# Two third sums on VectorE, one instruction each in place of three, and a new written order of the jobs

## The chip, the core and the metric

The kernel runs on one core of a Trainium2 chip. The metric is the device time of one execution in microseconds, the median of several runs. TensorE (PE in the profile) multiplies matrices, VectorE (DVE) and ScalarE (ACT) work on elements, GpSimd (POOL) and SyncE (SP) mostly issue DMAs here.

## The reference

Two independent parts are written side by side into one output of 2048 rows and 2 x 576 columns.

```
q, k, v = split(x @ wqkv)                       # 32 heads of 18 columns
logits[s, w] = q[s] . k[s - 2w] / sqrt(18)      # w = 0..7, masked where s < 2w
a = softmax_w(logits) ; A = (sum_w a[s, w] v[s - 2w]) @ wo
kv = (k shifted and weighted by 4 taps) * v     # B's own q, k, v
y  = irfft(rfft(pad(kv)) * rfft(pad(ssm_k)))[:2048] + kv * ssm_D
B  = q * y
out = concat(A, B)
```

## The kernel before

Part A is a local dilated attention, part B a long convolution by transforms. The convolution is cut into 4 blocks of 512 rows. Each block of x (the product kv) and each block of the filter is turned into a spectrum by matmuls with tables of sines; the spectra of x lie in the tile `xw`, those of the filter in `Ks`. A spectrum has a real and an imaginary half of 2304 columns. A complex product is made with three real products instead of four, so each spectrum also needs a third half, the sum of its first two. For blocks 0 and 1 VectorE makes this third sum (`third_sum`, L939, instruction at L942); for blocks 2 and 3 DMAs do it (`third`, L632: a copy issued on SP at L634, then an adding DMA on POOL at L626).

All work after a fixed start is cut into some 360 jobs. The string `ORDER` (L20 to L37) names them in the order in which their instructions are issued; each engine then executes its own instructions in that order, and waits where its operands or its targets are not ready. Nothing else sets the order. The jobs of which the prediction speaks:

- `q..`, `k..`, `v..`: projections of x (matmuls L322, L326, L333, L339; ScalarE copies the result from PSUM, L355). `T`: taps of block i on VectorE (L517 to L536). `M`: folding (L545, copy L548). `I`: a table (L397). `x i g h`: a unit of the spectrum of x (four matmuls L682, copy L684).
- `Fm`: folds filter block m (matmuls L602, two ScalarE copies L605 into `Ks`, then three adding DMAs on POOL at L607 to L610). `K m c g`: a unit of the filter's spectrum (matmuls L567 and L568, copy L618). `K.1.` reads what the copies L605 wrote, `K.0.` what the adding DMAs left.
- `RG`: ScalarE reorders a block of v's weights, loaded from HBM (L780).
- `L h u c`: VectorE multiplies q by shifted k (L706) into one of three homes (`LHOMES`), and `G h u c` sums over the columns of a head on TensorE (L720). `sm`: softmax.
- `D`: weights spread by DMA; `V n c`: VectorE weighs v (L813) into one of three homes (`VHOMES`), `A n c` adds over w on TensorE (L824, tail L838). `O`: output projection (L888, L880).
- `p j t i`: VectorE multiplies third t of the spectra of x block i and filter block j-i (L950) into one of five homes (`PHOMES`); `z j t i` adds it up on TensorE (L975) and with the last i the result is copied (L988, the very last one by VectorE, L986). `y`: joins two products (L958) for block 3. `i`, `b`, `g`: inverse transform (L1010, L1029), mirrored half (L1059, L1038), multiplication by q (L1075, L1020) and store.
- `ak`, `ax`: the third sums of filter and of x.

PSUM has four slots of two banks. They are handed out in turn (`slots`, L103): a new unit of matmuls takes the slot that was given back first, and must wait until ScalarE has copied what was in it. A home of a product may be written again only when TensorE has read it. A matmul that uses a part of the array (64 rows or columns, 32 columns, a quarter) has another tile shape than a full one; the shape changes often between jobs.

Of the kernel before, what the change touches and what calls it, by code (L numbers as in the profile page):

```python
# [17 lines left out]
PSUM = bass.MemoryType.PSUM  # L18

ORDER = """  # L20
    T0 k03a' T1 S1 k03b I1 k02a k02b Lk2 Lv2 I0 k00a' Lk3 Lv3 M01 X5 k00b q10a Ex q10b Lf3 T2 Lo3 q13a' q13b
    k10a k10b T3 k13a' Lf2 k13b q12a q12b N2 Lo2 k01a M10 k01b Lf1 M00 k11a k11b q11a M11 q11b Lf0 N3 Lw SV L001
    k12a M20 k12b x001 M21 x021 q24a x020 q24b x000 Lo1 k24a Fr Lo0 Z2 N1 RG3 k24b RG2 F3 RG0 F2 L000 K310 G000
    K311 K210 K211 L002 K313 G001 RG4 F1 G002 L003 G003 K302 L004 G004 K301 L010 K212 L011 K303 K213 K203 N0 F0
    L012 K200 K300 G010 L013 K201 K312 K202 RG1 G011 G012 K113 K103 G013 L014 G014 K112 K102 K101 L100 K100 K010
    K111 K110 sm0a K001 K013 sm0b v24a' L101 v24b L102 G100 L103 G101 K012 sm0c sm0d U3 U2 K000 K011 K003 G102
    K002 D0 D1 v11a v11b G103 L104 G104 ak00 M30 v12a' v12b ak02 v01a ak01 L110 G110 M31 L111 G111 v01b v00a'
    L112 G112 L113 Wl v00b G113 x031 U1 L114 G114 V04 v10a' v10b A04 sm1a sm1b v02a v02b v03a' sm1c v03b x201
    V10 V11 sm1d V12 A10 v13a' v13b D2 x330 x310 x301 V13 A11 V20 V21 x200 x331 x230 x010 x221 A20 x321 V22 x210
    x011 V23 D3 V34 ax02 x220 x030 x300 D4 A21 V40 V41 A34 D5 O000' x211 V42 x320 x231 x111 x131 Tx2 A40 V43  # L30
    x120 x101 ax00 x130 ax01 V50 x121 x311 O001 A41 V51 O100' p000 x100 x110 O010 A50 V52 z000 O011' V53 O101
    A51 Tk2 p010 z010 ax10 O020' O021 p020 z020 O110' ak10 i000 p200 i02880 Q0 p100 z100 p101 p110 p111 Q1 z101
    i02881 i001 p121 p120 O111 z110 p201 z111 z120 p210 z121 O120 p211 z200 z210 z211 p212 z212 z201 p202 z202
    Tx3 p220 Tk3 p221 O030' p222 O121 b0288 z220 p301 z221 O031' p302 b00 z222 p303 i200 i100 g0 Q2 p300 y300
    p312 i12880 i201 i101 i12881 z300 z301 z303 p310 p311 y310 O130 b10 b1288 p313 g1 Q3 p322 O131' z310 p320
    z311 p321 z313 i22880 i300 b20 y320 p323 i22881 i301 b2288 g2 z320 z321 z323 b30 i3384L g30 g3384
"""  # L37

LHOMES = (0, 1, 2, 0, 1, 2, 0, 1, 2, 0, 1, 2, 0, 1, 0, 1, 0, 1, 0, 1)
# [6 lines left out]
def view(t, offset, dims):  # L46

    return bass.AP(tensor=t.tensor, offset=t.offset + offset, ap=[list(t.ap[0])] + [list(d) for d in dims])
# [3 lines left out]
def kernel(  # L52
# [42 lines left out]
    HB = 4 * D  # L95
    QTR = 768
# [15 lines left out]
    xw = main.tile([128, 12 * HB], BF16, name="xw")  # L112
# [5 lines left out]
    XG = (9, 0, 3, 6)  # L118
# [49 lines left out]
    Ks = main.tile([128, 12 * HB], BF16, name="Ks")  # L168
# [3 lines left out]
    def k_at(m, part):  # L172
        return 3 * HB * (3 - m) + HB * part
# [87 lines left out]
    for h in range(2):  # L261
        f = fold[:, 64 * h:64 * h + 64]
# [225 lines left out]
    def job(name, fn, *args):  # L488

        assert name not in jobs  # L490
        jobs[name] = partial(fn, *args)
# [444 lines left out]
    todo = [(j, t, i) for j in range(NBL) for t in range(3) for i in range(j + 1)]  # L936
    PRODUCT = (("av", 0), ("v", 6912), ("qk", 9216), ("qk", 9216 + HB), ("Ks", k_at(3, 2)))

    def third_sum(t, at, w):  # L939

        a, b, c = (view(t, at + HB * part, [[1, w]]) for part in range(3))
        tt(c, a, b, ALU.add)  # L942

    def product_home(n):
# [148 lines left out]
    for j in range(NBL):  # L1093
        job(f"Q{j}", load_q, j)
        for c0, n in ((0, HD), (HD, HD)) if j < NBL - 1 else ((0, 2 * TH), (2 * TH, TH)):
            inverse(j, c0, n)
    for t in range(3):
        job(f"ak0{t}", third_sum, Ks, k_at(0, 0) + QTR * t, QTR)
        job(f"ax0{t}", third_sum, xw, HB * XG[0] + QTR * t, QTR)
    job("ak10", third_sum, Ks, k_at(1, 0), HB)  # L1100
    job("ax10", third_sum, xw, HB * XG[1], HB)

    for name in ORDER.split():
        jobs.pop(name.rstrip("'"))(*([True] if name[-1] == "'" else []))
# [31 lines left out]
```

## Time and profile before

| what | value |
|---|---|
| runs shown | 206.28, 206.78, 206.79 us (median 206.78) |
| the profiled execution | 206.3 us, of which the span on the core is 204.6 us |
| granted TensorE clock, mean | 0.994 |
| PE matmuls busy | 196.9 us, 96% of the span, 2074 instructions |
| DVE busy | 192.3 us, 94%, 146 instructions |
| ACT busy | 155.6 us, 76% |
| POOL busy | 60.8 us, 30% |
| DMA | 38.48 MB, mean 188 GB/s |

Times in the views run from the start of the span. A row of the timeline has its start, how long it lasted, engine, line, operation, what is written and read, how many instructions are merged into it, and in brackets the idle time before it with what ended that. An engine's instructions overlap a little at their ends, so what a step costs on a busy engine is read from start to start. Matmuls are pipelined and their ends are modelled, so for PE the starts count too.

### The profile page before, as it was taken

The page shows a single profiled execution, that of the slowest core. Times are in us where ns is not written, and L with a number is a line of the kernel's source. Part 1 is how long each engine was busy: PE and PEld are TensorE (multiplying, and loading weights), DVE is VectorE, ACT ScalarE, POOL GpSimd, SP SyncE. Part 2 cuts the span into 40 slices and gives each one's busy share as a digit, 9 for nine tenths or more (in the row PEclk, how much of TensorE's full clock was granted, in tenths as well). Part 3 has the DMA queues.
Part 4 walks back from the last instruction along what each step waited for, and adds up shares of the span by engine and source line. Part 5 has one row for each costly group of instructions (what it writes and reads, how often), then busy time and mean ns, then how long its engine had stood idle before and what let it go on. Part 6 is the DMA issues. An engine that isn't in the chain of part 4 may idle for free.

```text
span 204.6 us, 5004 instructions
## 1 busy us (share of the span) xinstructions
PE 196.9 (96%) x2074; PEld 109.9 (54%) x2074; DVE 192.3 (94%) x146; ACT 155.6 (76%) x223; POOL 60.8 (30%) x106
## 2 busy tenths in 40 slices
PE   7999999999989999999999999999999999999990
PEld 2543544334455646543245556776666767766660
DVE  7559999999999999999999999999999999899992
ACT  4788995678899999966578678886778767767760
POOL 8989500011348581400380000004090001030300
PEclk9999999999999999999999999999999999999997
DMA  6999899989509869999899990879989303944555
GB/s 197 280 293 306 175 289 373 214 177 281 169 3 146 111 82 185 167 180 222 157 235 216 248 244 34 141 183 334 186 227 233 100 28 122 227 130 145 153 182 150
DMA packets 34916, 38.48 MB, mean 188 GB/s; under 512 B 17523, under 2 KB 28911, under 8 KB 34894
## 3 DMA queue, kind: packets, MB, share of 16 engines
q1 hardware_dynamic: 26668, 24.29, 46.5%
q0 software_dynamic: 5760, 11.36, 29.5%
q10 hardware_dynamic: 2466, 2.51, 3.6%
q8 instruction: 16, 0.26, 0.5%
q14 instruction: 6, 0.05, 0.1%
HBM read 13.11 MB, written 4.72 MB: 87 GB/s over the span
## 4 chain that ended last, share of the span: by engine, by line
PE 88%; DMA 3%; ACT 2%; DVE 2%; issue 1%; SPq 1%; DVEq 0%
PE ps_proj L322 18%; PE ps_fx L682 8%; PE ps_wo L888 8%; PE ps_z L975 8%; PE ps_inv L1010 7%; PE ps_acc L824 7%; PE ps_fk L567 5%; PE ps_log L720 5%; DMA Ks<-in_A_x_dram 3%; PE ps_proj L333 3%; PE ps_proj L326 3%; PE ps_proj L439 3%; PE ps_fk L568 3%; PE ps_fold L545 2%; PE ps_wo L880 1%
## 5 line engine op out<-in xcount | busy, mean ns | idle before, releaser
L322 PE MATMUL ps_proj<-xw 128*128 128x512 bf16 x160 | 38.5, 380 | 0.0
L706 DVE TENSOR_TENSOR av<-qk 128x4096 bf16<-128x4096 bf16 (+1 forms) x16 | 31.7, 2014 | 0.1
L322 PEld LDWEIGHTS <-xw 128*128 128x128 bf16 x160 | 13.9, 98 | 19.4 <-issue 5.7
L988 ACT ACTIVATE av<-ps_z 128x768 bf16<-128x768 f32 x23 | 17.2, 811 | 6.5 <-PE ps_z L975 6.0
L517 DVE TENSOR_TENSOR tB<-kj,skb 128x4608 bf16<-128x4608 bf16 (+1 forms) x8 | 19.3, 2416 | 0.1
L950 DVE TENSOR_TENSOR qk<-xw,Ks 128x2304 bf16<-128x2304 bf16 x14 | 18.9, 1354 | 0.3 <-PE ps_z L975 0.3
L684 ACT ACTIVATE xw<-ps_fx 128x576 bf16<-128x576 f32 x32 | 18.6, 665 | 0.3 <-PE ps_fx L682 0.2
L618 ACT ACTIVATE Ks<-ps_fk 128x576 bf16<-128x576 f32 x32 | 18.6, 699 | 0.2 <-PE ps_fk L568 0.2
L355 ACT ACTIVATE qk<-ps_proj 128x1024 bf16<-128x1024 f32 x14 | 14.3, 1023 | 5.2 <-PE ps_proj L333 2.8
L888 PE MATMUL ps_wo<-qk 128*128 128x288 bf16 x128 | 17.9, 287 | 0.0
L626 POOL DMA_DIRECT2D Ks<-Ks x8 | 10.1, 1426 | 26.0 <-PE ps_back L1059 19.3
L682 PE MATMUL ps_fx<-xw,TB 128*128 128x288 bf16 x128 | 17.7, 287 | 0.0
L567 PE MATMUL ps_fk<-Ks,TB 128*128 128x384 bf16 x62 | 16.5, 327 | 0.1
L824 PE MATMUL ps_acc<-av,ident 64*64 64x512 bf16 x160 | 15.3, 378 | 0.0
L1010 PE MATMUL ps_inv<-av,TI 128*128 128x288 bf16 (+1 forms) x112 | 15.2, 292 | 0.0
L568 PE MATMUL ps_fk<-Ks,TB 128*128 128x192 bf16 x62 | 15.2, 246 | 0.0
L682 PEld LDWEIGHTS <-TB 128*128 128x128 bf16 x128 | 11.9, 98 | 5.9 <-issue 2.7
L888 PEld LDWEIGHTS <-qk 128*128 128x128 bf16 x128 | 11.7, 98 | 5.4 <-issue 2.7
L355 ACT ACTIVATE v<-ps_proj 128x1024 bf16<-128x1024 f32 x9 | 9.3, 1033 | 6.5 <-PE ps_proj L322 4.5
L813 DVE TENSOR_TENSOR av<-Ks,v 128x4096 bf16<-128x4096 bf16 x6 | 13.5, 2286 | 0.0
L827 ACT ACTIVATE qk<-ps_acc 128x1024 bf16<-128x1024 f32 x8 | 8.2, 1024 | 6.7 <-PE ps_acc L824 6.7
L1010 PEld LDWEIGHTS <-TI 128*128 128x128 bf16 x112 | 10.6, 98 | 4.2 <-issue 1.1
(195 smaller groups left out, 441.6 us busy)
## 6 DMA issues: line engine op xcount, KB each, us to landing
Ks<-Ks POOLq DMA_DIRECT2D x8, 576.0 KB, 7.8
TB<-av SPq DMA_DIRECT2D x12, 256.0 KB, 5.4
kj<-in_B_k_dram SPq DMA_DIRECT2D x6, 504.0 KB, 7.0
vt<-in_B_v_dram SPq DMA_DIRECT2D x8, 288.0 KB, 5.3
Ks<-av SPq DMA_DIRECT2D x8, 256.0 KB, 5.6
out_dram<-qk ACTq DMA_DIRECT2D x5, 288.0 KB, 3.7
Ks<-in_A_x_dram SPq DMA_DIRECT2D x2, 576.0 KB, 5.4
xw<-in_A_wqkv_dram SPq DMA_DIRECT2D x2, 576.0 KB, 6.2
```

The lines of the kernel that those rows point to most:

```text
L322: nc.tensor.matmul(ps[:, jp, :], wq(kb, comp, 128 * ct, 128), xT(kb, 1024 * jj + 512 * jp, 512), **se)
L355: nc.scalar.activation(view(t, o + pad + 1024 * jj, [[512, 2], [1, 512]]), ps[:], ACT.Copy)
L517: tt(to, view(kj, row * D, [[D, n], [D, 4], [1, D]]), view(skb, row * D, [[D, n], [0, 4], [1, D]]), ALU.mult)
L567: nc.tensor.matmul(o[:, 0:2], w, rhs[:, 0:2], start=start, stop=stop)
L568: nc.tensor.matmul(o[:, 2], w, rhs[:, 2], start=start, stop=stop)
L618: nc.scalar.activation(view(Ks, k_at(m, cs ^ (m & 1)) + 96 * gi, [[768, 3], [384, 2], [1, 96]]), acc3(ps), ACT.Copy, scale=(PSG, MSG)[cs][ ...
L682: nc.tensor.matmul(ps[:, pm, 0:HD], TX[:, 2 * pm + c, 128 * gi:128 * gi + 128], kv[:, 2 * c + pm, HD * h:HD * h + HD], start=(c == 0), sto ...
L706: tt(view(P, at, [[step, 4], [256, nj], [1, 256]]), view(t, o + 256 * hh, [[0, 4], [512, nj], [1, 256]]), view(tk, ok + 2 + 8 * ug + 256 * ...
L824: nc.tensor.matmul(acc[64 * o:64 * o + 64, h, :], ident[64 * h:64 * h + 64, 64 * h:64 * h + 64], view(P[s], 256 * u, [[2048, 2], [1, 256]] ...
L888: nc.tensor.matmul(ps[:, r, 0:HD], oT(hh, j + 2 * r, t)[:, o:o + 128], wo[:, t // 2, t % 2, HD * h:HD * h + HD], start=(t == 0 and not fli ...
L950: tt(product_home(n), view(xw, HB * XG[i] + QTR * t, [[HB, 3], [1, QTR]]), view(Ks, k_at(j - i, 0) + QTR * t, [[HB, 3], [1, QTR]]), ALU.mult)
L1010: nc.tensor.matmul(ps[:, c, 0:n], TI[:, sl, pm, 128 * c:128 * c + 128], Yall(j % 2, pm, sl, slice(c0, c0 + n)), start=(pm == 0 and sl == 0 ...
```

## The change

`third_sum` always sums a whole half of 2304 columns. For block 1 it did so before. For block 0 the sum was cut into three pieces of 768 columns (`ak00`, `ak01`, `ak02` of the filter, `ax00`, `ax01`, `ax02` of x), each a job of its own; now there is one job each, `ak00` and `ax00`. VectorE has four instructions less; what is computed is the same. The string `ORDER` is written anew, with the same jobs otherwise.

```diff
-    T0 k03a' T1 S1 k03b I1 k02a k02b Lk2 Lv2 I0 k00a' Lk3 Lv3 M01 X5 k00b q10a Ex q10b Lf3 T2 Lo3 q13a' q13b
+    T0 k02a I1 S1 k01a' k01b k03a' k03b k02b k00a' k00b X5 k11a M01 T1 Lk2 Lv2 T2 Ex Lk3 q11a q11b k13a k13b
...
-    def third_sum(t, at, w):
-
-        a, b, c = (view(t, at + HB * part, [[1, w]]) for part in range(3))
+    def third_sum(t, at):
+
+        a, b, c = (view(t, at + HB * part, [[1, HB]]) for part in range(3))
         tt(c, a, b, ALU.add)
...
-    for t in range(3):
-        job(f"ak0{t}", third_sum, Ks, k_at(0, 0) + QTR * t, QTR)
-        job(f"ax0{t}", third_sum, xw, HB * XG[0] + QTR * t, QTR)
-    job("ak10", third_sum, Ks, k_at(1, 0), HB)
-    job("ax10", third_sum, xw, HB * XG[1], HB)
+    for j in range(2):
+        job(f"ak{j}0", third_sum, Ks, k_at(j, 0))
+        job(f"ax{j}0", third_sum, xw, HB * XG[j])
```

The queues of DMA issues on SP and POOL keep their order, but for two neighbours on POOL (L579 and the last L650). The order moves on PE, ACT and VectorE, at these places above all.

First, ScalarE where the last projections end and the filter begins. L355 is a copy of a projection (the first is q24, the second k24), L684 one of a unit of x, L548 of a fold of x, L780 the reordering of weights (`RG`), L605 the copies of a filter fold, L618 those of units of the filter's spectrum. Before:

```order
L684 ACTIVATE xw<-ps_fx 128x2x3x96 x2
L355 ACTIVATE qk<-ps_proj 128x1024
L684 ACTIVATE xw<-ps_fx 128x2x3x96
L780 ACTIVATE xw<-Ks 128x576
L355 ACTIVATE qk<-ps_proj 128x1024
L780 ACTIVATE xw<-Ks 128x576
L605 ACTIVATE Ks<-ps_rev 128x576 x2
L780 ACTIVATE xw<-Ks 128x576
L605 ACTIVATE Ks<-ps_rev 128x576 x2
L618 ACTIVATE Ks<-ps_fk 128x6x96 x5
L780 ACTIVATE xw<-Ks 128x576
```

And now:

```order
L684 ACTIVATE xw<-ps_fx 128x2x3x96 x2
L548 ACTIVATE xw<-ps_fold 128x576 x2
L355 ACTIVATE qk<-ps_proj 128x1024
L780 ACTIVATE xw<-Ks 128x576 x2
L355 ACTIVATE qk<-ps_proj 128x1024
L780 ACTIVATE xw<-Ks 128x576
L605 ACTIVATE Ks<-ps_rev 128x576 x4
L618 ACTIVATE Ks<-ps_fk 128x6x96 x6
L780 ACTIVATE xw<-Ks 128x576
L605 ACTIVATE Ks<-ps_rev 128x576 x2
```

Before, two reorderings stood between the copy of q24 and the first fold's copies, and a third between the two folds; now all three stand ahead of both folds, two of them ahead of the copy of k24. On TensorE, one filter unit (K310) stood between the second fold and the first sum of pair products (G000); now there are three (K311, K312, K313).

Second, VectorE around the filter's third sum of block 0 (L942). L756 ends the first softmax, L706 are pair products, the 2048 wide one ahead of the sum is L104, the next 4096 wide one L110, and L813 is the first weighing of v. The piece of the difference, before with -, now with +:

```order
 L756 TENSOR_TENSOR av<-av 128x2048
 L706 TENSOR_TENSOR av<-qk 128x2048
-L942 TENSOR_TENSOR Ks<-Ks 128x768 x3
-L706 TENSOR_TENSOR av<-qk 128x4096 x4
+L706 TENSOR_TENSOR av<-qk 128x4096 x3
+L942 TENSOR_TENSOR Ks<-Ks 128x2304
+L706 TENSOR_TENSOR av<-qk 128x4096
 L706 TENSOR_TENSOR av<-qk 128x2048
 L813 TENSOR_TENSOR av<-TB,v 128x4096
```

The sum no longer stands between L104 and L110, but three pair products later.

Third, VectorE where the second half of the attention is weighed, with the third sum of x. The TB row is V34, the first Ks rows are V40 and V41 in either order:

```order
 L813 TENSOR_TENSOR qk<-qk,v 128x4096
 L813 TENSOR_TENSOR av<-TB,v 128x4096
-L942 TENSOR_TENSOR xw<-xw 128x768
-L813 TENSOR_TENSOR av<-Ks,v 128x4096
 L813 TENSOR_TENSOR qk<-Ks,v 128x4096
-L813 TENSOR_TENSOR av<-Ks,v 128x4096 x2
-L942 TENSOR_TENSOR xw<-xw 128x768 x2
+L813 TENSOR_TENSOR av<-Ks,v 128x4096 x3
+L942 TENSOR_TENSOR xw<-xw 128x2304
 L813 TENSOR_TENSOR qk<-TB,v 128x4096
```

Before, a third of the sum stood between V34 and V40; now V41 follows V34 at once, V40 comes after it, and the whole sum stands behind V43.

In the last part the products change places too: `p200` moves behind `p120`, `p220` to `p222` keep their places, `p303` comes ahead of `p302`, `g1` ahead of `p313`, and `y320` directly behind `p322`, with `p321` after it.

More of the change, by code (lines that the diff above doesn't have):

```diff
@@ L20 @@
 ORDER = """
-    T0 k03a' T1 S1 k03b I1 k02a k02b Lk2 Lv2 I0 k00a' Lk3 Lv3 M01 X5 k00b q10a Ex q10b Lf3 T2 Lo3 q13a' q13b
[L22 to L35, printed above, removed]
@@ L36 @@
-    z311 p321 z313 i22880 i300 b20 y320 p323 i22881 i301 b2288 g2 z320 z321 z323 b30 i3384L g30 g3384
+    T0 k02a I1 S1 k01a' k01b k03a' k03b k02b k00a' k00b X5 k11a M01 T1 Lk2 Lv2 T2 Ex Lk3 q11a q11b k13a k13b
+    q12a' q12b M11 k11b Lv3 T3 Lf3 k10a' Lo3 q13a q13b Lf2 Lo2 M00 k10b q10a' q10b Lf1 Lo1 k12a' M21 k12b x000
+    x001 q24a I0 M20 N2 x021 x020 Lf0 Lo0 N3 M10 q24b Lw RG2 SV RG4 Fr Z2 L002 k24a k24b RG3 F3 F2 K311 K312 N1
+    L000 K313 L001 G000 L003 K212 K211 K210 G001 G002 L004 RG0 F1 K300 G003 L010 L011 K302 K310 K303 G004 K213
@@ new lines @@
+    K200 K203 N0 F0 G010 K201 K202 L012 K301 RG1 L013 G011 G012 U3 K113 K110 L014 L100 G013 G014 sm0a K111 L101
+    K102 K101 K011 K103 K012 K112 sm0b L102 K010 v24a' v24b K100 G100 L103 G101 sm0c K003 sm0d K001 K000 G102
+    L104 K002 K013 D0 x031 v01a G103 G104 L110 L111 M31 v01b v11a' G110 v12a' v12b U2 L112 ak00 D1 v11b G111
+    L113 G112 Wl U1 M30 v00a' v00b G113 L114 x030 G114 v10a v10b V04 A04 sm1a sm1b v02a v02b v03a' V11 sm1c v03b
+    V10 x201 A10 v13a sm1d v13b x310 x330 x311 V12 V13 D2 V20 A11 x221 x301 x011 x231 x331 V21 A20 V22 x321 V23
@@ new lines @@
+    x320 x230 x210 D3 D4 x200 A21 V34 D5 x211 x010 O000 A34 x220 Tx2 x130 x111 V41 V40 A40 x131 V42 V43 Tk2 x101
+    x121 x120 x300 ax00 V50 O001 A41 O100' x110 x100 O010' V51 A50 p000 z000 O011' V52 V53 O101 A51 p010 Q0 ak10
+    z010 O020' O021 p020 z020 O110' Q1 p110 i000 i02880 ax10 p100 z100 p101 z101 p111 p121 i02881 p120 p200 Tx3
+    i001 O111 z120 z121 z110 p210 p201 z111 O120' z200 p211 p212 z210 z211 z212 p202 z201 z202 p220 p221 b0288
+    O030' O121 z220 Tk3 p222 z221 z222 O031' p301 p303 p302 b00 i12880 g0 i100 i200 i101 p300 y300 p312 i12881
@@ L37 @@
+    i201 z300 b10 z301 b1288 p310 O130' Q2 p311 y310 O131' g1 z303 p313 i22880 z310 p320 z311 z313 i22881 i300
+    b2288 b20 Q3 p322 y320 p321 p323 i301 g2 z320 z321 z323 b30 i3384L g30 g3384
 """
```

## The prediction

> **What bounds the kernel now.** I read the page's busy times first, then the merged timeline of each engine where they meet, and the chain that ended last.
>
> ```profile
> PE 196.9 (96%) x2074; PEld 109.9 (54%) x2074; DVE 192.3 (94%) x146; ACT 155.6 (76%) x223; POOL 60.8 (30%) x106
> ...
> 56.00:63.00 7.00, 6.25 (x51) 4.15 (x50) 7.00 (x5) 6.99 (x11) 3.97 (x6) 1.00 0.28 42
> 63.00:128.00 65.00, 65.00 (x647) 33.60 (x648) 64.64 (x44) 53.46 (x80) 19.48 (x21) 1.00 0.88 171
> 162.00:180.00 18.00, 17.83 (x298) 12.71 (x287) 16.70 (x14) 12.83 (x20) 1.21 (x1) 1.00 0.44 124
> ```
>
> The columns of the stages after the length are PE, PEld, DVE, ACT and POOL busy, then the granted clock. Two engines are nearly full everywhere. TensorE idles 0.75 us from 56 to 63 and not at all from 63 to 128; VectorE has 1.3 us of idle time from 162 to 180, and 0.36 in the 65 us from 63 to 128. So the time is TensorE's work plus its waits, with VectorE just ahead of it or just behind.
>
> The last stretch shows who holds whom:
>
> ```profile
> 166.17 1.36 DVE L950 TENSOR_TENSOR Ks<-xw,Ks 128x2304 bf16<-128x2304 bf16 x1
> ...
> 169.13 1.36 DVE L950 TENSOR_TENSOR v<-xw,Ks 128x2304 bf16<-128x2304 bf16 x1 [0.33 <-PE ps_z L975]
> ...
> 176.00 1.36 DVE L950 TENSOR_TENSOR qk<-xw,Ks 128x2304 bf16<-128x2304 bf16 x1 [0.25 <-PE ps_z L975]
> ...
> 179.03 1.36 DVE L950 TENSOR_TENSOR av<-xw,Ks 128x2304 bf16<-128x2304 bf16 x1 [0.41 <-DMA Ks<-Ks]
> 180.42 1.36 DVE L958 TENSOR_TENSOR av<-av,qk 128x2304 bf16<-128x2304 bf16 x1
> ...
> 165.94 0.33 PE L975 MATMUL ps_z<-qk,identn 64*64 64x384 bf16 x4
> ...
> 167.58 0.36 PE L975 MATMUL ps_z<-Ks,ident 64*64 64x384 bf16 x4 [0.17 <-DVE Ks L950]
> ...
> 168.23 0.36 PE L975 MATMUL ps_z<-v,identn 64*64 64x384 bf16 x4
> ...
> 168.47 0.47 SPq L634 DMA_DIRECT2D Ks<-Ks  x1
> 173.00 1.21 POOL L626 DMA_DIRECT2D Ks<-Ks  x1 [19.30 <-PE ps_back L1059]
> ```
>
> The product at 166.17 is p212. Its home in `Ks` was read by z200, whose last matmuls are over at about 166.1 (z210 begins at 165.94, and a matmul of 0.33 overlaps the next by half): VectorE wrote as soon as it could. Its sum z212 starts at 167.58, when the product is done, and ends when z201 begins (168.23) plus some 0.2. Then SP copies into the same place (168.47), POOL adds (173.00), and p300 waits for the landing (179.03). From p300 on VectorE has 13 instructions without idle time up to p323, and the chain ends behind that:
>
> ```profile
> 193.24 1.35 DVE L958 TENSOR_TENSOR av<-av,qk 128x2304 bf16<-128x2304 bf16 x1
> 194.50 1.35 DVE L950 TENSOR_TENSOR qk<-xw,Ks 128x2304 bf16<-128x2304 bf16 x1
> ...
> 194.69 1.80 PE ps_z L975 x40
> 196.51 0.82 ACT av L988
> ```
>
> TensorE begins z320 some 0.1 us after y320 ends (193.24 plus 1.35), and z323 needs p323 (194.50 plus 1.35, 195.85). Both engines arrive together. So the end hangs on z200 through p212, z212, the DMAs and p300; VectorE's own work before 162 does not reach it.
>
> **The change part by part.** Sums are made against the profiled execution, 206.3 us (span 204.6 and 1.7 around it), which is 0.48 below the median of the runs shown.
>
> *Four instructions less.*
>
> ```profile
> 89.91 1.49 DVE L942 TENSOR_TENSOR Ks<-Ks 128x768 bf16<-128x768 bf16 x3
> 91.32 10.08 DVE L706 TENSOR_TENSOR av<-qk 128x4096 bf16<-128x4096 bf16 x5
> ...
> 151.79 1.35 DVE L942 TENSOR_TENSOR Ks<-Ks 128x2304 bf16<-128x2304 bf16 x1
> 153.06 1.35 DVE L950 TENSOR_TENSOR Ks<-xw,Ks 128x2304 bf16<-128x2304 bf16 x1
> ```
>
> From start to start the three pieces take 1.41 us (89.91 to 91.32), one whole sum 1.27 (151.79 to 153.06): 0.14 saved, twice, 0.28 us of VectorE. The pieces stand before 130 us; from 162 on VectorE waits for TensorE's reads of the products, as at 169.13, so what it gains earlier it would lose there. On the path I cost it at nothing. If VectorE led nowhere, it would be worth its full 0.28.
>
> The Trainium skill (Perfetto Trace Analysis, Identifying the Most-Contended Engine) says that matmul busy time is no good measure and that the engine with the highest occupancy should be worked on; by it TensorE has room (54% weight loads) and VectorE, 94% busy, would be the bound, so the sum would be -0.28. The rows above, where VectorE waits for TensorE, speak against it; it stands among the rivals.
>
> *TensorE's own work.* The matmuls are the same, only changes of tile shape are more or fewer.
>
> ```profile
> 88.35 1.89 PE L322 MATMUL ps_proj<-xw 128*128 128x512 bf16 x8
> 90.18 0.39 PE L333 MATMUL ps_proj<-xw 64*128 64x512 bf16 x2
> 90.50 1.05 PE L720 MATMUL ps_log<-av,E 128*32 128x512 bf16 x16
> ```
>
> A pair of L333, which runs side by side, is followed by another shape 0.32 us after its start (90.18 to 90.50). Eight L322 take 1.83 to the next shape (88.35 to 90.18); with 0.32 for the last, the other seven take 0.216 each. So a change of shape costs 0.10 us. Counted through the order there are 133 before and 136 now: five fewer up to the filter folds, given back until the attention's second half, one more up to z200, and two more after it. Up to z200 that is +0.1; the two after it lie where TensorE waits for p323, with 0.1 to spare at z320, so +0.1 at most, which goes with the last term.
>
> *The place from 53 to 63 us.* Here TensorE waits, and the new order moves the most.
>
> ```profile
> 53.23 1.02 ACT L355 ACTIVATE qk<-ps_proj 128x1024 bf16<-128x1024 f32 x1 [0.69 <-PE ps_proj L339]
> 54.15 0.65 ACT L684 ACTIVATE xw<-ps_fx 128x576 bf16<-128x576 f32 x1
> ...
> 56.93 1.28 ACT L780 ACTIVATE xw<-Ks 128x576 bf16<-128x576 bf16 x1
> 58.12 1.16 ACT L605 ACTIVATE Ks<-ps_rev 128x576 bf16<-128x576 f32 x2
> 59.18 1.25 ACT L780 ACTIVATE xw<-Ks 128x576 bf16<-128x576 bf16 x1
> ...
> 58.84 0.33 PE L567 MATMUL ps_fk<-Ks,TB 128*128 128x384 bf16 x1
> ...
> 59.33 0.32 PE L567 MATMUL ps_fk<-Ks,TB 128*128 128x384 bf16 x1
> ...
> 60.36 0.61 PE L720 MATMUL ps_log<-av,E 128*32 128x512 bf16 x8 [0.62 <-DVE av L706]
> 61.02 0.32 PE L567 MATMUL ps_fk<-Ks,TB 128*128 128x384 bf16 x1
> ...
> 63.23 0.62 PE L720 MATMUL ps_log<-av,E 128*32 128x512 bf16 x8
> 63.77 0.42 PE L602 MATMUL ps_rev<-Ks,flip2r 128*128 128x288 bf16 x2
> ```
>
> Before: K310 starts at 58.84, its second pair waits for the second copy of the fold (59.33 in place of 59.08), then G000 waits for L000 (60.36 in place of 59.67): 0.25 and 0.69, together 0.94 us. Then come the other units and G001, and at 63.77 the next fold.
>
> Now TensorE comes to the folds about 0.5 earlier (five shapes fewer), and so does q24's copy, at 53.3 beside a rather full ScalarE. Behind it stand, from start to start of the rows: q24 0.92 (53.23 to 54.15), two L780 of 1.19 (56.93 to 58.12), k24 another 0.92, L780 1.19, the first fold's copies 1.06 (58.12 to 59.18). That puts the first fold's copies at 58.7 to 59.75, and the second's, 1.06 behind, to 60.8. K311 can begin at 59.25 and end at 60.0; TensorE is through with the folds at 58.35. So it waits 0.9 and 0.35 before and in K311; K312 and K313 follow to 61.0, G000 at 0.54 (it now begins after the 60.36 at which L000 was there before) to 61.55, three more units of 0.49 (58.84 to 59.33) to 63.1, G001 and G002 at 0.54 each (63.23 to 63.77) to 64.1. Before, five units and two sums were done at 63.77; the sixth unit and third sum are worth 0.49 and 0.54, and TensorE's lead takes 0.5 off, which gives 64.3. That comes out even within 0.2: 0, and between -0.94 (the wait covered whole) and +0.4 (ScalarE late by a third of an L780). I take 0, since the wait for L000 is replaced by one for the fold's copies. K300 and K302 now come earlier behind the fold whose copies and adding DMAs they need; that they wait for these is part of the +0.4.
>
> *The third sums moved.* Three things are queued behind each other on VectorE there.
>
> ```profile
> 125.31 2.29 DVE L813 TENSOR_TENSOR av<-TB,v 128x4096 bf16<-128x4096 bf16 x1
> 127.51 0.55 DVE L942 TENSOR_TENSOR xw<-xw 128x768 bf16<-128x768 bf16 x1
> 127.98 2.28 DVE L813 TENSOR_TENSOR av<-Ks,v 128x4096 bf16<-128x4096 bf16 x1
> ...
> 127.73 1.04 PE L838 MATMUL ps_acc<-av,ident 64*64 64x256 bf16 x32
> ```
>
> V40 overwrites a home that A21 reads; A21's matmuls end just past 127.73, and V40 began at 127.98. The piece of the sum between them was that wait, used. Now V41 comes straight after V34, at 127.37, into a home of A21 too: it waits up to 0.45. Likewise L110 now follows L104 at 89.91 (where the three pieces began) and must wait until G103 has read L103. G103 began at 90.50, behind a whole projection (2.15 from 88.35); now half of one and a unit of x stand there (together some 1.5), and four changes of shape less (0.4), so it reads from 89.4 to 90.0: L110 waits 0.1, at most 0.4. Both waits are mostly paid from the 0.28 and from what TensorE itself is behind. I put 0 on the path and keep +0.6 for the range.
>
> *The end.* y320 now follows p322, which it reads. Such a step starts 1.39 after (179.03 to 180.42) where others take 1.27: +0.12 between p300 and p323, which nothing hides. p303 ahead of p302 removes the 0.25 before 176.00, but p300 waits for its DMA all the same.
>
> Sum: +0.1 (shapes to z200), 0, 0, +0.1 (y320): +0.2, so 206.5 for an execution like the profiled one and 206.78 + 0.2 = 207.0 for the median. About 0.3%, 0.6 us, is what a measurement of this kernel can tell from no change.
>
> **The rivals.**
>
> *The wait at 56 to 63 is covered.* If the first fold's copies come by 58.4, K311 to K313 fill what was lost to L000. For it: ScalarE's 0.69 of idle time ahead of 53.23 shows that it could start earlier. Against: two L780 now stand ahead of k24's copy. Price -0.94: 206.0; with VectorE's 0.28 on top 205.8.
>
> *VectorE is the bound.* Then the 0.28 reaches the end and the shapes don't: 206.5, within what can't be told. Against: the waits of VectorE above.
>
> *The spacing is lost.* If A21 ends later than V34 (127.37 on VectorE's axis), V41 waits 0.45, and with L110's 0.4 VectorE falls 0.6 behind after its 0.28; A51 began the moment V53 was done, so TensorE, z200 and the DMA chain follow. Price +0.6 on top of 0.2: 207.6; with ScalarE's 0.4 at 60 us 208.0. It decides from 0.3 us on, where VectorE's lead is spent.
>
> **How the numbers follow.** Forecast 0.48 (within 0.3%, the second rival's 0.1 with it); the wait covered 0.22 (faster); the spacing lost, or ScalarE late at the folds, 0.30 (slower). The range goes from 205.8 to 208.0, the bounds of the two outer cases.
>
> **What would show it.** Right: L942 twice at some 1.35 without pieces; TensorE still waiting about 1 us between 58 and 61, now before L567 and not L720; SP's L634 for `Ks` at 168 to 169 and p300 held by its DMA near 179; VectorE without waits from there to p323. Wrong: K311 starting at once behind the folds (faster), idle time of VectorE at 90 or 127 and of TensorE at 132 or 148 (slower), or p300 not held by its DMA at all.

## The result, and the profile after

The changed kernel takes 208.36 us (median; 208.16 to 209.06), the kernel before 206.78 beside it: a ratio of 1.0093, 95% interval 1.007 to 1.0116. It is slower by some 1.6 us, under 1% but clear of the interval. The forecast was 207.0 with a range up to 208.0, so the time lies outside it, on the slow side.

The profiled execution took 208.43 us, its span 206.7 (before: 206.3 and 204.6), 2.1 us more than the one before. A second group of runs (new_order_again, below) gave 2.3 us more by its medians; the losses that are added up below are those of the profiled executions. First its busy times and the three stretches that the prediction showed:

```profile
PE 197.6 (96%) x2074; PEld 109.5 (53%) x2074; DVE 192.5 (93%) x142; ACT 155.6 (75%) x223; POOL 61.4 (30%) x106
```

```profile
56.00:63.00 7.00, 6.05 (x52) 3.71 (x50) 5.78 (x5) 7.00 (x11) 2.32 (x4) 1.00 0.01 1
63.00:128.00 65.00, 65.00 (x632) 33.51 (x634) 63.82 (x40) 53.77 (x80) 21.04 (x23) 1.00 0.92 175
162.00:180.00 18.00, 17.84 (x305) 12.59 (x303) 17.02 (x14) 12.91 (x20) 1.19 (x1) 1.00 0.42 117
```

VectorE, third after the length, has lost its lead: it idles 1.2 us from 56 to 63 and again 1.2 from 63 to 128. But these are not where the time goes, as the experiments show. The waits that matter begin earlier. TensorE's timeline at the place where the projections of q end, and where the filter begins:

```profile
49.31 0.61 PE L397 MATMUL ps_ti<-ident,TB 128*64 128x128 bf16 x16
49.76 0.66 PE L545 MATMUL ps_fold<-xw,fold 128*64 128x288 bf16 x8
51.10 1.19 PE L682 MATMUL ps_fx<-xw,TB 128*128 128x288 bf16 x8 [0.69 <-ACT TI L401]
...
54.30 1.92 PE L326 MATMUL ps_proj<-xw 128*64 128x512 bf16 x16
...
60.46 0.32 PE L567 MATMUL ps_fk<-Ks,TB 128*128 128x384 bf16 x1 [0.81 <-ACT Ks L605]
...
62.31 0.62 PE L720 MATMUL ps_log<-av,E 128*32 128x512 bf16 x8
```

and ScalarE's beside it:

```profile
49.96 1.08 ACT L401 ACTIVATE TI<-ps_ti 128x512 bf16<-128x512 f32 x2 [0.19 <-PE ps_ti L397]
...
58.58 1.29 ACT L780 ACTIVATE xw<-Ks 128x576 bf16<-128x576 bf16 x1
59.74 2.28 ACT L605 ACTIVATE Ks<-ps_rev 128x576 bf16<-128x576 f32 x4
```

L397 is I0, a table for the inverse transforms. On TensorE's timeline of before it stood here, and the next jobs found a slot without a wait:

```profile
23.08 0.64 PE L397 MATMUL ps_ti<-ident,TB 128*64 128x128 bf16 x16
```

Now I0 stands between q24 and M20. The unit of x that follows is given I0's slot of PSUM, and waits 0.69 us until ScalarE has copied it (49.96 plus 1.08). ScalarE began these two copies at once: it had been idle for 0.19 us until I0 was done. That wait is new, and the prediction does not have it. K311's wait for the fold's copies (0.81, then 61.00 in place of 60.70) is the one it does have.

VectorE's waits, the first for G000, the second for G103:

```profile
62.98 3.43 DVE L706 TENSOR_TENSOR av<-qk 128x4096 bf16<-128x4096 bf16 x2 [1.22 <-PE ps_log L720]
...
91.27 6.70 DVE L706 TENSOR_TENSOR av<-qk 128x4096 bf16<-128x4096 bf16 x3 [0.72 <-PE ps_log L720]
97.88 1.35 DVE L942 TENSOR_TENSOR Ks<-Ks 128x2304 bf16<-128x2304 bf16 x1
```

And the stretch from z212 to z300:

```profile
168.67 0.36 PE L975 MATMUL ps_z<-Ks,ident 64*64 64x384 bf16 x4 [0.17 <-DVE Ks L950]
169.56 0.47 SPq L634 DMA_DIRECT2D Ks<-Ks  x1
174.00 1.19 POOL L626 DMA_DIRECT2D Ks<-Ks  x1 [19.22 <-PE ps_wo L880]
180.75 1.36 DVE L950 TENSOR_TENSOR av<-xw,Ks 128x2304 bf16<-128x2304 bf16 x1 [0.91 <-DMA Ks<-Ks]
183.55 0.36 PE L975 MATMUL ps_z<-av,ident 64*64 64x384 bf16 x4 [0.54 <-DVE av L958]
```

z212, SP's copy and POOL's adding DMA each come 1.0 to 1.1 later than before. But from POOL's issue to p300 there are now 6.75 us (174.00 to 180.75), before 6.03 (173.00 to 179.03); and from p300 to the last step of VectorE 21.32 (180.75 to 202.07), before 20.89 (179.03 to 199.92).

The two orders have done the same work of TensorE when they come to k24, to K113, to z212 and to the end, so the loss can be read there. The executions differ in their start by up to some 1 us (last section), and that has to come off: the start is read at an L322 near the beginning, for the new order the one at 18.32 here, for the order of before the one at 20.92. The two profiles themselves start alike: the last x8 group of L439, which comes ahead of all jobs in both, begins at 15.96 here and at 15.94 before. A table of such losses, in us later than before with the difference of the start taken off, serves the experiments too:

| ready to begin | changed kernel | old_front | new_front | new_middle | old_tail |
|---|---|---|---|---|---|
| k24 (54) | 0.60 | 0 | 0.59 | 0 | 0.60 |
| K113 (75) | 0.69 | 0.03 | 0.69 | 0.04 | 0.69 |
| z212 (168) | 1.09 | 0.43 | 0.92 | 0.44 | 1.09 |
| p300 (180) | 1.72 | 0.80 | 0.83 | 0.26 | 0.95 |
| VectorE's last step (201) | 2.15 | 1.23 | 0.83 | 0.34 | 0.99 |
| start taken off | 0 | 0.71 | 0.26 | -0.34 | 0.62 |

Each column is one execution.

### The profile page after: what moved, and what is told of

Same layout as the page of the kernel before. It is cut to its first block, busy times and chain, and to the rows that moved or that the text cites. A ratio compares the mean times of both kernels' runs of the same rounds, so it can differ in the third digit from the quotient of the medians.

```text
span 206.7 us, 4997 instructions
## 1 busy us (share of the span) xinstructions
PE 197.6 (96%) x2074; PEld 109.5 (53%) x2074; DVE 192.5 (93%) x142; ACT 155.6 (75%) x223; POOL 61.4 (30%) x106
## 4 chain that ended last, share of the span: by engine, by line
PE 86%; ACT 4%; DVE 4%; DMA 3%; issue 1%; DVEq 0%
PE ps_proj L322 18%; PE ps_fx L682 7%; PE ps_wo L888 7%; PE ps_acc L824 7%; PE ps_z L975 6%; PE ps_fk L567 5%; PE ps_log L720 5%; PE ps_inv L1010 4%; PE ps_proj L439 3%; DMA Ks<-Ks 3%; PE ps_proj L333 3%; PE ps_proj L326 3%; PE ps_fk L568 3%; PE ps_fold L545 2%; PE ps_rev L602 2%; PE ps_sk L453 2%
## 5 line engine op out<-in xcount | busy, mean ns | idle before, releaser
L322 PE MATMUL ps_proj<-xw 128*128 128x512 bf16 x160 | 38.7, 380 | 0.0
L706 DVE TENSOR_TENSOR av<-qk 128x4096 bf16<-128x4096 bf16 (+1 forms) x16 | 31.7, 2015 | 1.9 <-PE ps_log L720 1.9
L322 PEld LDWEIGHTS <-xw 128*128 128x128 bf16 x160 | 13.9, 98 | 19.7 <-issue 6.3
L355 ACT ACTIVATE qk<-ps_proj 128x1024 bf16<-128x1024 f32 x14 | 14.4, 1027 | 6.8 <-PE ps_proj L322 3.9
L618 ACT ACTIVATE Ks<-ps_fk 128x576 bf16<-128x576 f32 x32 | 18.9, 682 | 0.3 <-PE ps_fk L568 0.2
L684 ACT ACTIVATE xw<-ps_fx 128x576 bf16<-128x576 f32 x32 | 18.7, 666 | 0.1
L626 POOL DMA_DIRECT2D Ks<-Ks x8 | 10.9, 1638 | 25.4 <-PE ps_wo L880 19.2
L355 ACT ACTIVATE v<-ps_proj 128x1024 bf16<-128x1024 f32 x9 | 9.2, 1033 | 5.9 <-PE ps_proj L322 3.7
L813 DVE TENSOR_TENSOR av<-Ks,v 128x4096 bf16<-128x4096 bf16 x6 | 13.5, 2284 | 0.0
```

Source lines behind the costliest of these rows:

```text
L322: nc.tensor.matmul(ps[:, jp, :], wq(kb, comp, 128 * ct, 128), xT(kb, 1024 * jj + 512 * jp, 512), **se)
L355: nc.scalar.activation(view(t, o + pad + 1024 * jj, [[512, 2], [1, 512]]), ps[:], ACT.Copy)
L618: nc.scalar.activation(view(Ks, k_at(m, cs ^ (m & 1)) + 96 * gi, [[768, 3], [384, 2], [1, 96]]), acc3(ps), ACT.Copy, scale=(PSG, MSG)[cs][ ...
L706: tt(view(P, at, [[step, 4], [256, nj], [1, 256]]), view(t, o + 256 * hh, [[0, 4], [512, nj], [1, 256]]), view(tk, ok + 2 + 8 * ug + 256 * ...
```

## Experiments: the instruction or the order

The theories, by the letters that the expectations use. **A**: VectorE sets the pace, and its waits at 62 and 90 us are the loss. **B**: TensorE sets it, VectorE only where it feeds it. **C**: the time is lost behind z200. **D**: the wait for I0's slot at 51 us is the root, all later waits its echo. **E**, formed after D's size failed: several losses of TensorE in series, each carried to the end. **F** and **G** belong to single runs.

Line numbers in some of these kernels are one lower than above, because the string of the order is a line shorter. The kernel before ran beside each group of runs, with medians of 206.4 to 206.5 us there.

**whole_old_order.** The kernel of before, each cut sum made whole at the place of its last piece.

```diff
- L104 G104 ak00 M30 v12a' v12b ak02 v01a ak01 L110
+ L104 G104 M30 v12a' v12b v01a ak00 L110
- V34 ax02 x220
+ V34 x220
- x101 ax00 x130 ax01 V50
+ x101 x130 ax00 V50
```

> The order of before, with each of the two cut sums made whole at the place of its last piece: the four instructions less, alone. Theory A (VectorE sets the pace up to the inverse transforms): its 0.28 us reach the end, 206.5 us against 206.8 of before. Theory B (TensorE sets the pace, VectorE only where it feeds it): no difference, 206.8. Theory C (the time is lost behind z200, in the DMAs and the last products): as B.

Measured: 206.49 us, ratio 1.0008 (0.999 to 1.0026). No difference, as B and C had it; A's 0.28 us less is just outside the interval. VectorE's timeline shows a wait that was not there:

```profile
128.00 2.29 DVE L812 TENSOR_TENSOR av<-Ks,v 128x4096 bf16<-128x4096 bf16 x1 [0.35 <-PE ps_acc L823]
```

V40, which before began at 127.98 without a wait, now waits 0.35 us for A21 and begins at the same time. Before, a piece of the sum filled this wait; now that piece has to be done behind V43. So VectorE comes later to V53, in spite of its 0.28 us less work (before, and here):

```profile
145.66 2.29 DVE L813 TENSOR_TENSOR qk<-TB,v 128x4096 bf16<-128x4096 bf16 x1
```

```profile
145.96 2.28 DVE L812 TENSOR_TENSOR qk<-TB,v 128x4096 bf16<-128x4096 bf16 x1
```

With the 0.06 by which this execution starts later taken off, that is 0.24. TensorE's jobs begin as before up to there; A53, which needs V53, comes 0.23 later at 148 us and z212 0.24, and 0.13 is left at the end. The time does not show it. So here a delay of VectorE does reach TensorE.

**pieces_new_order.** The changed kernel's order with the sums in three pieces again (`ak00 ak02 ak01`, `ax02 ax00 ax01` where the whole ones stand).

> The new order, with the sums cut into three pieces again, all three at the place of the whole one: the order alone. All theories expect the loss to stay: A 208.6 us (VectorE has 0.28 more to do), B and C 208.4. If the whole sum itself were the cause, 206.8.

Measured: 208.83 us, ratio 1.0121 (1.0092 to 1.0149). All theories expected it: the order alone makes all of the loss.

## Experiments: which part of the order

Up to K113 both orders hold the same jobs (but for `U3`), so they can be joined there; and from p202 on again.

**old_front, new_front, new_middle, old_tail.** Whole sums in all four.

```diff
 old_front   order of before up to K113, then U3 and the new order
 new_front   new order up to K113, then the order of before
 new_middle  before up to K113, new to p202, before from there
 old_tail    new order up to p202, then the order of before
```

> Whole sums; the order of before up to K113 (75 us, where both orders have done the same work), the new order behind it. Theory E (three losses in series on TensorE, each carried to the end unchanged: 0.69 us up to K113, 0.4 from there to z212, 1.06 behind it): 1.46 us above before, about 207.9. Theory A (VectorE's waits at 62 and 90 are the loss): without the wait at 62, and with TensorE earlier at 90, only the tail is left, 207.5.

> Whole sums; the new order up to K113, the order of before behind it. Theory E: 0.69 us above before, about 207.15. Theory A: VectorE, 0.55 behind at K113 with 1.27 still to do for the sum, catches up at no cost if TensorE leads there, else 207.0. If the slack of the old order took it up: 206.5.

> Whole sums; the order of before up to K113 and from p202 on, the new order between them: the third sums moved, without what stands ahead and behind. Theory E: 0.4 us above before, about 206.85. The prediction's third rival (spacing lost by the moved sums): 207.1 or more.

> The new order up to z212, and from there the order of before. Theory C: between z212 and the end the new order lost 0.63 us up to p300 (the adding DMA took 6.72 us instead of 6.01) and 0.43 behind it, so 1.06 goes: about 207.4 us beside 208.5. Theory D alone: 208.5, the tail is only moved along. If it is both, C's gain here and D's in the run beside it are to be added up.

Measured: old_front 208.18 us, ratio 1.0086 (1.0057 to 1.0114). new_front 207.40, 1.0041 (1.0022 to 1.006). new_middle 206.82, 1.0014 (0.9998 to 1.003). old_tail 207.82, 1.0058 (1.0034 to 1.0082). The columns of the table above show the same in parts: the front costs 0.69 us wherever it is new and nothing where it is old, the new middle 0.40, the tail some 0.8 to 1.2. The parts add up to 1.9 to 2.3, beside 2.15 for the whole: this is theory E, three losses in series. In new_front the old middle loses 0.23 too: that is the loss of whole sums in the order of before, as in whole_old_order. With the old tail 0.1 us of what was lost up to z212 is not seen at the end. The times alone show less: that the front and the tail lose something (new_front; old_front beside new_middle), while new_middle can't be told from no loss, nor from the third rival's 207.1. E's three forecasts (207.9, 207.15, 206.85) lie inside the intervals. Theory A's 207.5 for old_front lies just outside its interval, and its picture does not fit the trace: old_front's wait at 91 us, on VectorE's timeline, is there although TensorE comes to G103 without the front's delay:

```profile
91.31 6.70 DVE L705 TENSOR_TENSOR av<-qk 128x4096 bf16<-128x4096 bf16 x3 [0.83 <-PE ps_log L719]
```

In the middle TensorE's timeline shows no new wait. Changes of tile shape fit its loss, though no run tried them alone: from K113 to z212 there are 55 in the timeline of before and 60 in that of after, at the 0.10 us that the prediction measured 0.5, beside 0.40 found.

## Experiments: the front, and VectorE's waits

**ak_early.** The changed kernel, `ak00` moved to between G104 and L110.

> The new order with the whole third sum of the filter between L104 and L110, where the pieces were. VectorE's wait of 0.72 us ahead of L110 is then filled with work that has to be done anyway. Theory A: 207.65 us. Theory B: 208.4, TensorE's order is the same. Theory C: 208.4, or as A if z200 follows VectorE.

Measured: 209.06 us, ratio 1.0122 (1.0094 to 1.0149): nothing gained, against A's 207.65. The wait ahead of L110 is gone, but VectorE's timeline has others:

```profile
98.97 3.43 DVE L705 TENSOR_TENSOR av<-qk 128x4096 bf16<-128x4096 bf16 x2 [0.48 <-PE ps_log L719]
102.77 2.29 DVE L812 TENSOR_TENSOR av<-TB,v 128x4096 bf16<-128x4096 bf16 x1 [0.37 <-PE ps_log L719]
139.75 2.29 DVE L812 TENSOR_TENSOR qk<-TB,v 128x4096 bf16<-128x4096 bf16 x1 [0.72 <-DMA TB<-av]
```

0.48 and 0.37 for TensorE's sums are together a little more than the 0.72 removed. The third, ahead of V50, is for a DMA that came late (last section); behind it TensorE is 0.80 us later than in the changed kernel, so the time of this run says little. The trace says more: from K113 up to 149 us, ahead of that loss, TensorE's jobs begin within 0.03 us of where they do in the changed kernel, start taken off. Filling the wait ahead of L110 gave TensorE nothing. Theory A falls here: this wait is an echo of TensorE's lateness.

**sums_early.** The changed kernel with the sums of the attention ahead of the units of the filter:

```diff
- F3 F2 K311 K312 N1 L000 K313 L001 G000 L003 K212 K211 K210 G001 G002 L004 RG0 F1
+ F3 F2 N1 L000 G000 K311 K312 K313 L001 G001 L003 G002 K212 K211 K210 L004 RG0 F1
```

> The new order with G000 ahead of the filter's units and G001, G002 earlier too, so that the homes of L000 and L001 come free sooner. Theory A: VectorE's 1.22 us wait ahead of L003 goes and reaches the end, 207.2 us. Theory B: TensorE has a sum of 0.55 to do while it waits for the fold's copies, 207.8. Theory C: nothing behind z200 is changed in order, so the chain moves with z200: whatever A or B say up to there, and 1.0 us stays lost behind it.

Measured: 209.38 us, ratio 1.0136 (1.0111 to 1.0162): no gain, where A and B both expected one; by the medians it is slower than the changed kernel (208.36 and 208.64), though the intervals overlap. The trace agrees with slower. With the difference of the start (0.76) taken off, its K113 comes 0.42 us later than the changed kernel's. VectorE's wait at 62 is gone, but ScalarE now runs out of units to copy, which its timeline shows:

```profile
62.63 1.78 ACT L617 ACTIVATE Ks<-ps_fk 128x576 bf16<-128x576 f32 x3
65.11 1.74 ACT L617 ACTIVATE Ks<-ps_fk 128x576 bf16<-128x576 f32 x3 [0.69 <-PE ps_fk L567]
```

From 54 to 82 us ScalarE has next to no idle time, before or after. Here it loses 0.69 us, and TensorE's next units, which wait for its copies, come late.

**table_early and table_early_old_tail.** The changed kernel with I0 behind k02 again; the second with the tail of before as well.

```diff
- k03a' k03b k02b k00a' k00b
+ k03a' k03b k02b I0 k00a' k00b
- x001 q24a I0 M20 N2 x021
+ x001 q24a M20 N2 x021
```

> The new order with only I0 moved back, from behind q24 to behind k02, where ScalarE has time. Theory D (the loss starts at 51 us, where a unit of x waits for the slot that I0's copies hold: 0.69 us of TensorE, and all that follows is only its echo): the wait goes and TensorE reaches z200 0.7 us earlier, so about 207.8 us beside 208.5 for the new order as it was. Theory A (VectorE's own waits at 62 and 90 are the loss): they remain in part, 0.2 to 0.4 us gained. Theory C (only what lies behind z200 counts): no difference.

> Both of them: I0 early and the tail of before. If the two losses stand in series, 208.5 - 0.7 - 1.06 = 206.7 us, the time of before. If one hides the other, 207.4.

Measured: table_early 208.77 us, ratio 1.0114 (1.0078 to 1.015), nothing that the runs can tell; table_early_old_tail 207.12, 1.003 (1.0009 to 1.005), beside old_tail's 207.82: 0.7 less, as D said, but the intervals of the two overlap. The trace of table_early tells more: its start is 0.84 late and k24 0.57, so 0.27 us is gained, and z212 keeps it (0.27). Theory D has the right place and the wrong size. Of the wait of 0.69, some 0.2 comes back because I0 now stands between jobs of other tile shapes (it costs some 0.7 us there and 0.45 beside M20), and some 0.3 because the second unit of x then begins 0.80 behind the first in place of 0.49.

**table_late_old_order.** The kernel of before with only I0 moved behind x001.

```diff
- k02b Lk2 Lv2 I0 k00a'
+ k02b Lk2 Lv2 k00a'
- k12b x001 M21 x021 q24a
+ k12b x001 I0 M21 x021 q24a
```

> The order of before, sums in pieces, with only I0 moved to behind x001, so that the next jobs find its slot still held. Theory D: the same wait of some 0.7 us on TensorE as in the new order, and it reaches the end: 207.1 to 207.5 us against 206.8. Theory A: VectorE leads there by more than that, no difference, 206.8.

Measured: 206.65 us, ratio 1.001 (0.9991 to 1.0029). The wait is there on TensorE's timeline, but shorter:

```profile
51.38 0.84 PE L325 MATMUL ps_proj<-xw 128*64 128x512 bf16 x6 [0.33 <-ACT TI L400]
```

Start taken off, k24 comes 0.23 later and VectorE's last step 0.17. The time can't tell that from nothing, and D's 207.1 is missed; the trace goes with D in kind.

## Experiments: the tail, and what else is tight

**new_order_again, b0_back, tail_first_part.** The changed kernel itself as a measure, and two with a part of its tail restored:

```diff
 b0_back
- b0288 O030' O121 z220
+ O030' O121 b0288 z220
 tail_first_part
- p220 p221 b0288 O030' O121 z220 Tk3 p222 z221 z222 O031' p301 p303 p302 b00
+ p220 Tk3 p221 O030' p222 O121 b0288 z220 p301 z221 O031' p302 b00 z222 p303
```

> The changed kernel itself once more, as the measure for the two runs beside it that restore parts of its tail. All theories: 208.4 to 208.6 us.

> The new order with only b0288 moved back behind O030 and O121, so that their two stores start 0.3 to 0.5 us earlier against z212 and the adding DMA. Theory G1 (the DMA takes 6.72 instead of 6.01 us because it now shares its time with those two stores): 0.3 to 0.6 us less than the new order. Theory G2 (the DMA's length is chance, or comes from the later order around p303): no difference.

> The new order with the jobs from p220 to z222 as before, and the end behind p300 left new. If the loss of 0.63 us up to p300 lies in these jobs and that of 0.43 behind p300 in the end's own order: 0.6 us less than the new order, and 0.4 more than with the whole tail of before. If the end alone counts: no difference.

Measured: new_order_again 208.64 us, ratio 1.0108 (1.0082 to 1.0133); b0_back 208.28, 1.0077 (1.005 to 1.0104); tail_first_part 208.61, 1.0098 (1.0073 to 1.0122). The adding DMA and p300 in new_order_again:

```profile
173.44 1.19 POOL L625 DMA_DIRECT2D Ks<-Ks  x1 [18.92 <-PE ps_wo L879]
...
180.68 1.36 DVE L949 TENSOR_TENSOR av<-xw,Ks 128x2304 bf16<-128x2304 bf16 x1 [1.09 <-DMA Ks<-Ks]
```

and in b0_back:

```profile
173.89 1.19 POOL L625 DMA_DIRECT2D Ks<-Ks  x1 [19.32 <-PE ps_back L1058]
...
179.96 1.36 DVE L949 TENSOR_TENSOR av<-xw,Ks 128x2304 bf16<-128x2304 bf16 x1 [0.33 <-DMA Ks<-Ks]
```

Issued 0.45 later, it lands 0.72 earlier. With the starts taken off (both begin 0.2 to 0.3 us before the changed kernel's first profile), b0_back is 0.6 ahead of that one at p300 and at the end. Over the profiled executions, regroup_pool's left out, the DMA took 6.41 to 7.21 us in the seven with b0288 ahead of O030, and 5.86 to 6.26 in the ten with it behind. So with one job of 0.25 us of TensorE put ahead of two output units, a transfer takes some 0.7 us longer. That it shares its time with the stores of those units, which then start later, was G1's reason. It is not shown, and one run speaks against it: tail_first_part has its store 0.3 us behind the adding DMA's issue, much as the changed kernel has, and its DMA takes 6.13. The traces give G1's size; the times, 208.28 beside 208.64, lie the same way, but their intervals overlap. The reason is open.

tail_first_part gains too and gives it back. Its V50 waited 0.54 us for a DMA, so that it comes to z212 0.62 us later than the changed kernel, start taken off; at p300 it is 0.30 ahead. Then it takes 22.0 us from p300 to VectorE's last step, against 21.32 or 21.33 in the eight executions with the new end whole and 20.89 to 21.02 in the eight with that of before. In the time there is no difference to new_order_again, as was expected if the end alone counted; by the trace it is a gain and two losses. That the end costs 0.43 by itself, as was expected of it, stands by those two figures and old_tail: the one that joins old jobs to the new end does not measure it.

**sum_twice.** The kernel of whole_old_order, with the filter's sum computed a second time behind the first (the same values are written).

> The order of before with whole sums, and the filter's sum of block 0 computed twice in a row (the second writes the same values): 1.27 us more for VectorE at 91 us, nothing else. Theory A (VectorE sets the pace): 1.1 to 1.3 us more, 207.6 to 207.8. Theory E (TensorE sets it; in the order of before it comes to G113 0.5 us after L113 is done): what is over that slack, 0.6 to 0.8 us more, 207.1 to 207.3. If VectorE is not bound at all: 206.5.

Measured: 207.27 us, ratio 1.0041 (1.0024 to 1.0058): 0.8 above whole_old_order. E's range was 207.1 to 207.3; A's 207.6 lies just outside the interval. Of 1.27 us, 0.5 was slack, and then TensorE waits, on its timeline at G111:

```profile
97.08 0.61 PE L719 MATMUL ps_log<-av,E 128*32 128x512 bf16 x8 [0.54 <-DVE av L705]
```

So theory E holds on this side too. VectorE is here no more than 0.5 us from being the bound: taking 0.28 from it changes nothing in the time, adding 1.27 costs 0.8.

**regroup_pool.** The kernel of whole_old_order, two of five reorderings of weights on GpSimd.

```diff
+        if kb in (0, 1):
+            nc.gpsimd.tensor_copy(view(xw, w_at(kb, 2), [[64, 9], [1, 64]]), view(raw, D * kb, [[1, 9], [9, 64]]))
+        else:
             nc.scalar.activation(view(xw, w_at(kb, 2), [[64, 9], [1, 64]]), view(raw, D * kb, [[1, 9], [9, 64]]), ACT.Copy)
```

> The order of before with whole sums, and two of the five reorderings of v's weights (RG0, RG1) done by GpSimd instead of ScalarE. ScalarE has no idle time from 53 to 84 us, and TensorE's units of the filter go at its pace there. Theory F (ScalarE sets the pace of that stage): 1.2 to 2.4 us less work for it, 0.5 to 2 us faster than before, 204.5 to 206.0. If TensorE or VectorE is as full as it there: 206.5. GpSimd's copy may also hold up the filter's adding DMAs behind it: then 207 or more.

Measured: 219.08 us. One of the six runs took 209.06 us, the other five 217.56 to 219.68; all are above the slowest run of the kernel before beside them, 207.16. So it is slower, by 2.5 us or by 11 to 13. The profile is of one of the five, and what differed in the one run is not known. GpSimd's copies there, each of which ScalarE does in some 1.3 us:

```profile
61.69 11.40 POOL L780 COPY xw<-Ks 128x576 bf16<-128x576 bf16 x1
...
83.04 4.46 POOL L780 COPY xw<-Ks 128x576 bf16<-128x576 bf16 x1
```

and VectorE's work at that time:

```profile
69.74 2.27 DVE L705 TENSOR_TENSOR av<-qk 128x4096 bf16<-128x4096 bf16 x1
82.25 4.18 DVE L705 TENSOR_TENSOR v<-qk 128x4096 bf16<-128x4096 bf16 x1 [10.24 <-PE ps_log L719]
```

The filter's next adding DMAs stood behind the first copy on POOL's queue, and everything behind those. The run says nothing on theory F for the time; only that the first fold's units did come a us earlier (ScalarE copied them from 60.42 on, before from 61.40).

None of the kernels tried is faster than the kernel before. The one that keeps what the change was about, whole_old_order, has the same time.

## Why the prediction was wrong

**What bounds the kernel: right, but not taken far enough.** TensorE's work plus its waits sets the time, with VectorE just ahead of it. whole_old_order (1.0008) and sum_twice (0.8 of 1.27) bear that out, against the rival that VectorE is the bound. That rival stood beside a rule of the Trainium skill (Perfetto Trace Analysis, Identifying the Most-Contended Engine: work on the engine with the highest occupancy); here VectorE, 94% busy, gave nothing in the time for 0.28 us less work. What the prediction did not draw from it: what TensorE loses before 168 us reaches the end, all but some 0.1 us. The prediction let two losses there be paid from leads that don't exist.

**Four instructions less: right.** Nothing in the time. At the places of the last pieces, in the order of before, the whole sums even cost 0.24 us at z212 by the trace, since V40's wait stands empty.

**TensorE's own work: the sum failed.** The price of 0.10 us for a change of shape was good. But the count was used only up to z200 (+1 in all, 0.1 us), with the five that are saved first set off against those spent later. Between K113 and z212 they are spent, and 0.40 us is found there. The saving at the front, four changes by the two timelines, shows only as 0.09 (0.69 of wait, 0.60 of loss); where the other 0.3 went was not told apart.

**The place from 53 to 63 us: the step that failed.** "Now TensorE comes to the folds about 0.5 earlier" is wrong: it comes 0.60 later. Of these 1.1 us, 0.69 is the wait at 51 us; the rest is the saving in shapes that did not show. From there on the working was good. The units wait for the fold's copies and not for L000, 0.81 and 0.30 in place of 0.9 and 0.35, and the place comes out even (0.60 ahead of it, 0.69 behind). What was missed lies just ahead: I0 moved by 26 us, from where the next jobs found a slot without a wait to where a unit of x is given I0's own, still being copied. The prediction followed what moves at the place, not what had moved into the way to it. What this wait costs by itself is less than its row: with I0 back at its old place, the trace of table_early gains 0.27 of the 0.69. L003's wait of 1.22 for G000 was not foreseen either; old_front has no wait of that size there (0.52 and 0.46 us at 64 and 66), and its loss in the middle is the same 0.40.

**The third sums moved: right that these waits cost nothing here, wrong in their size.** L110 waits 0.72, not 0.1 to 0.4: G103 begins at 90.60, not at 89.4, and only 0.66 of that is the front's delay (in old_front, without it, L110 waits 0.83). V41 does not wait at all, since VectorE is later still. Neither is the cost: ak_early removed the first and gained nothing. The loss of the middle, which the third rival priced at 0.6, is 0.40; the five changes of shape fit it, which is argued and not shown.

**The end: the step that failed second.** That p300 is held by its DMA was right, and so was y320 straight behind p322 (193.80 after 192.42, 1.38). But the DMA's length was taken from the row of before, 6.0 us, though the new order moves jobs past it. It took 6.72, and in the other execution of the same kernel 7.21. And the end behind p300 lost 0.43, not 0.1 to 0.2. Up to the last full-width product it is 0.13, y320's share as forecast; the rest lies in VectorE's last rows, here and before, with a longer wait for the mirrored half:

```profile
202.07 1.02 DVE L1020 TENSOR_TENSOR TB<-ps_back,TB 128x384 bf16<-128x384 f32 x2 [0.78 <-PE ps_back L1038]
```

```profile
199.92 1.02 DVE L1020 TENSOR_TENSOR TB<-ps_back,TB 128x384 bf16<-128x384 f32 x2 [0.59 <-PE ps_back L1038]
```

**The rivals.** The wait covered: not so, 0.81 stands. VectorE the bound: no. The slower one came nearest in sign, with the wrong mechanism for the changed kernel. Its path is real, though: in whole_old_order a late V53 makes A53 and z212 0.23 to 0.24 late.

## What to carry to other kernels

Where an engine is full, find every place at which the new order makes it wait, from the start, and add them up to the end: here a front that came 0.69 us late, 0.40 us in the middle and a longer transfer each came through nearly in full, and 0.28 us saved on the other full engine did not. Look at each job that moves far, however small it is, and ask what its copies or its slot meet where it lands. A transfer on the path is not to be taken at the length that it had: jobs that move past it can change it.

## What the runs showed of the hardware

**The start differs, and nothing takes it up.** The changed kernel and table_early have the same jobs up to here, on TensorE's timeline:

```profile
18.32 1.04 PE L322 MATMUL ps_proj<-xw 128*128 128x512 bf16 x4
```

```profile
19.16 1.04 PE L321 MATMUL ps_proj<-xw 128*128 128x512 bf16 x4
```

Over the executions this job began from 18.06 to 19.16 in the new order, and its counterpart from 20.59 to 21.87 in that of before. All of TensorE's later jobs then shift by the same amount (old_tail's by 0.62 at every job from 18 to 173 us). The scatter of the runs, some 0.7 to 1.8 us within one kernel (regroup_pool left out), may be mostly this.

**A transfer's length varies.** The last DMA that spreads weights into `TB` ahead of V50 took 8.20 to 8.38 us in ak_early, table_early_old_tail and tail_first_part, and 6.3 to 7.3 in the other profiled executions; only then did V50 wait, 0.54 to 0.72 us, and z212 came 0.6 to 0.8 us later. All three have the new order in the middle, but so have others that did not wait. The reason is open.

**GpSimd's copy and VectorE.** In the profiled execution of regroup_pool the first copy began at 61.69 beside VectorE at work without a pause, and ended at 73.09, 1.1 us after VectorE's last instruction there (69.74 plus 2.27). The second ran beside a product that took 4.18 us in place of 2.27. The Trainium skill (SBUF — State Buffer, "SBUF: two separate sides") says that VectorE and GpSimd share one pair of ports, under a lock that goes for a whole instruction to whichever starts first, while the other waits; a VectorE instruction with two inputs from SBUF counts against a GpSimd one that reads SBUF, as here. The first row agrees with that: the copy ended only when VectorE had stopped. The second agrees in part: the two did hold each other up, but the product had begun 0.79 us before the copy and was slowed all the same, which a lock held from its start does not explain.
